# A second MoE layer with seven products: work of the other engines reordered around the products, squares moved to ACT, last step of each pass plain

## The chip, the cores and the metric

The kernel runs on one core of a Trainium2 chip. The metric is the device time of one execution in microseconds; the median of three runs is given, and one more execution was profiled. PE is the matrix engine (PEld its weight loads), DVE, ACT and POOL are the vector, scalar and GpSimd engines, SP issues nearly all DMAs. Each engine, and SP's queue, works off its instructions in program order.

## The reference

```python
# attention with two head-mixing matrices, then two feed-forward layers on 1792 tokens
s = mix(softmax_input = scale * q @ k.T, w_pre);  a = mix(softmax(s), w_post);  x = a @ v
h = x @ moe_w_in                                   # 768 -> 1024
solu = h * softmax(h);  ln = (solu - mean) / std * g_ln
x2 = ln @ moe_w_out                                # 1024 -> 768
h = x2 @ moe2_w_in                                 # 768 -> 2048
r = np.maximum(h, 0.0);  g = r * r
out = g @ moe2_w_out                               # 2048 -> 768
```

The weights of both feed-forward layers arrive as 64-bit floats.

## The kernel before, in words

The program has four stages: attention; the first MoE (`h1`, `norm1`, `zt`, `out1`), in tiles of 128 tokens for the way in and groups of 384 for the way out; a last loop of ten `out1` without `h1`, beside which the second MoE's first data are prepared; and the second MoE, which the change is about. All fp32 products are made of three matmuls each: an operand is split into a high part (a rounding copy on ACT) and a low part (a subtraction on DVE or POOL), and hi·hi, hi·lo and lo·hi are summed in PSUM.

The 64-bit weights are narrowed to fp32 by `narrow`: one square on ACT (line 75) and four operations on DVE (76, 80, 84, 88) for each piece of 128 x 384, then a store to DRAM (737) and the load of the piece after the next. A second-MoE weight has 64 pieces. They are put in small portions between other work: each call of `filler()` issues one DVE operation. The square's scratch tile (`wsq`) has one buffer, so the square of a piece waits for line 88 of the piece before. A loop of the first MoE issues 12 fillers in one batch ahead of its two `out1`, the last loop 5 after each `out1`, and each step of the second MoE up to 8.

The second MoE works in two passes p over tokens, of 1024 and of 768, each in two token groups q (`GRP`: 512 and 512, then 512 and 256), and in each pass over eight blocks of 256 hidden columns. `it` counts the 16 blocks of both passes, `e` the one within its pass; a step is a pair (it, q). A step has two parts on PE:

- `h2(it, q)`: 2 hidden tiles f x 6 chunks x 3 = 36 matmuls (line 916) of 512 or 256 columns. Relu on ACT (924) and the square on DVE (925, reading PSUM again) give `r`.
- `y2(it, q)`: g is cut in 2 x 2 blocks (hidden tile x token half), the weight block in 2 x 2 (hidden tile x half of the 768 outputs). Instead of eight block products there are seven, of sums of blocks: `s1..s4` on POOL (943), `t1..t4` on DVE (889). Each of the seven is 6 matmuls of 384 columns (3 for the group of 256 tokens; line 1020) into one of three PSUM buffers, and is then added to an fp32 sum `y` in SBUF by DVE (1031), or copied by ACT where e is 0 (1029). At the end of a pass `join` (seven DVE additions per group, line 983) turns the seven sums into the four output blocks. Only the very last block, `plain(it)`, has eight products into four sums of two.

PE's order is h2 of the next step, then y2 of this one, and so on; `h2(next)` is issued with 4 fillers after each hidden tile. After it, still ahead of this step's y2, a step with q = 0 issues `sum_to` (four DVE subtractions), two `split_to` and the four `split_ti` (ACT copy 829, POOL 830) of the next block, for which only two raw buffers `tir` exist, so that two of their loads wait for the first two splits. Splits of g (954, 955) are issued with or after h2 for k = 0 and 1 and in the `hook` between products for the rest; the splits of `to` (897, 898) likewise for k = 2 and more. The tokens `x2` are loaded and split in two halves of three chunks (801, 802), those of the second pass during block 7; both `join`s of a pass are worked off in one stretch at the next step with q = 0.

Of the kernel before, what the change touches and what calls it, by code (L numbers as in the profile page):

```python
# [18 lines left out]
def kernel(  # L19
# [726 lines left out]
    for m in range(NTILE):  # L746
# [76 lines left out]
    def split_ti(it, j):  # L823
# [3 lines left out]
        hi, lo = [ti[it, f][:, a, 3 * s:3 * s + 3] for a in range(2)]  # L827
        r = tir.pop((it, j)).rearrange("p (c f) -> p c f", c=3)
        nc.scalar.copy(hi, r)  # L829
        nc.gpsimd.tensor_tensor(out=lo, in0=r, in1=hi.bitcast(F32), op=ALU.subtract)  # L830

    def ahead():

        load_ti(0, 0)
        load_ti(0, 1)
        for half in range(2):
            yield from part_x2(0, 0, half, wi2_p)
        for j in range(4):
# [9 lines left out]
    for i, (g, cc) in enumerate(outs):  # L848
# [22 lines left out]
    def load_to(it):

        b = []
        for j in range(4, 8):
            i = 8 * (it % NE) + j
            need(i + 1)
            t = m2_p.tile([128, HM], F32, tag="tor", name="tor", bufs=4)
            nc.sync.dma_start(out=t, in_=w2D[i * 128:(i + 1) * 128, :])
            b.append(t)
        bsrc[it] = b  # L880

    def sum_to(it):
        b11, b12, b21, b22 = bsrc[it]
# [4 lines left out]
        for o, x, y in ((t1, b12, b11), (t2, b22, t1), (t3, b22, b12), (t4, t2, b21)):  # L888
# [17 lines left out]
    def plain(it):  # L906
        return it == NI - 1

    def h2(it, q, nf):
        n = GRP[it // NE][q][1]  # L910
        rs = []
        for f in range(KE):
            ps = ps2_p.tile([128, 512], F32, tag="h", name="ps_h2", bufs=2)
            for cc in range(CC):
                for i, (w, a) in enumerate(((0, 0), (0, 1), (1, 0))):
# [3 lines left out]
                        rhs=x2[it // NE, q][cc // 3][:, a, cc % 3, 0:n],  # L919
# [25 lines left out]
        split_g(it, q, 0)  # L945
        split_g(it, q, 1)

    def split_g(it, q, k):
        if k >= len(gsrc[it, q]):
            return  # L950
        r = gsrc[it, q][k]
        w = GRP[it // NE][q][1] // 2
        t = m2_p.tile([128, 2, TG // 2], F32R, tag="g", name="g", bufs=9)[:, :, 0:w]
        nc.scalar.copy(t[:, 0], r)
        (nc.vector if k < 2 else nc.gpsimd).tensor_tensor(  # L955
            out=t[:, 1], in0=r, in1=t[:, 0].bitcast(F32), op=ALU.subtract
        )
        gs.setdefault((it, q), []).append(t)
# [10 lines left out]
    def join(p, q):  # L969
# [3 lines left out]
        done = {}  # L973
        for o, x, y, op, c in (
            (p2, p1, p2, ALU.add, (0, 0)),
            (p6, p1, p6, ALU.add, None),
            (p7, p6, p7, ALU.add, None),
            (p6, p6, p5, ALU.add, None),
            (p5, p7, p5, ALU.add, (1, 1)),
            (p4, p7, p4, ALU.subtract, (1, 0)),  # L980
            (p3, p6, p3, ALU.add, (0, 1)),
        ):
            nc.vector.tensor_tensor(out=o, in0=x, in1=y, op=op)
            if c:
                done[c] = o
                if p == 0:
                    store_y(p, q, *c, o)
            yield True
        ys[p, q] = done

    def y2(it, q, hook):
        p, e = divmod(it, NE)
        na = GRP[p][q][1] // 256
        g = gs.pop((it, q))
        if plain(it):
            for (i, u) in ((0, 0), (0, 1), (1, 0), (1, 1)):
                ps = ps2_p.tile([128, 2, 512], F32, tag="y", name="ps_y", bufs=3)
                ab = [((g[0], g[1]), (g[3], g[2]))[i], ((to[it][0], to[it][1]), (to[it][3], to[it][2]))[u]]
                for a in range(na):
                    for f, (gg, tt) in enumerate(zip(*ab)):  # L1000
                        for j, (ga, wa) in enumerate(((0, 0), (0, 1), (1, 0))):
                            nc.tensor.matmul(
                                out=ps[:, a, 0:HM],
                                lhsT=gg[:, ga, a * 128:(a + 1) * 128],
                                rhs=tt[:, wa],
                                start=(f == 0 and j == 0),
                                stop=(f == KE - 1 and j == 2),
                            )
# [3 lines left out]
                hook(2 * i + u)  # L1012
            return
        if e == 0:
            ys[p, q] = [m2_p.tile([128, 2, HM], F32, tag=f"y{q}_{k}", name="y") for k in range(7)]
        for k in range(7):
            ps = ps2_p.tile([128, 2, 512], F32, tag="y", name="ps_y", bufs=3)
            for a in range(na):
                for j, (ga, wa) in enumerate(((0, 0), (0, 1), (1, 0))):
                    nc.tensor.matmul(  # L1020
                        out=ps[:, a, 0:HM],
                        lhsT=g[k][:, ga, a * 128:(a + 1) * 128],
                        rhs=to[it][k][:, wa],
                        start=(j == 0),
# [17 lines left out]
    for k in range(2, 7):  # L1042
        split_g(0, 0, k)
# [98 lines left out]
```

## Time and profile before

| | us |
|---|---|
| median of 3 runs (lowest, highest) | 1401.6 (1400.91, 1402.68) |
| profiled execution / its span | 1401.2 / 1399.3 |
| PE busy | 1211.3 (87%) |
| DVE / ACT / POOL busy | 903.3 / 571.9 / 572.5 |
| chain that ended last | PE 71%, DVE 10%, DMA 5%, POOL 5%, ACT 4%, issue 4% |

The profile's rows are read like this. A group's row gives the busy time, the mean length of one, and the idle time of that engine right before such instructions with what ended it. A timeline row gives start and length of a run of like instructions, and in brackets the idle time before it. The granted clock (PEclk) is a mean over a stretch between half speed, 0.5 for 1.2 GHz, and full speed, 1.0 for 2.4 GHz.

### The profile page before, as it was taken

How to read it: one execution, taken by the hardware profiler on the slowest of the kernel's cores; microseconds unless marked ns; L12 is line 12 of the kernel's file. 1: busy time of each engine (PE TensorE's matmuls, PEld its weight loads, DVE VectorE, ACT ScalarE, POOL GpSimd, SP SyncE). 2: the span in 40 equal slices, each digit the busy share in tenths (PEclk: the TensorE clock that was granted, in tenths of full speed). 3: DMA queues.
4: the chain of work that ended last, by engine and by line, in shares of the span. 5: the costliest groups of instructions: out<-in, count | busy, mean ns of one | idle time of the engine just before them, and what ended most of it. 6: DMA issues, size and time to landing. Idle time of an engine off the chain costs nothing.

```text
span 1399.3 us, 22134 instructions
## 1 busy us (share of the span) xinstructions
PE 1211.3 (87%) x7587; PEld 1012.0 (72%) x7587; DVE 903.3 (65%) x1649; ACT 571.9 (41%) x1445; POOL 572.5 (41%) x741
## 2 busy tenths in 40 slices
PE   9999999999999999999775776867798758777787
PEld 4777777777777889999764665756687547777777
DVE  4776777677757677777456367676655573555557
ACT  4565556666655442232233523232322234333331
POOL 2332232242215341110126646465557565566651
PEclk9999999999999999999888788987999878889998
DMA  6766665765636244444465223231211241111111
GB/s 182 223 187 185 196 195 175 201 202 168 199 123 191 80 141 147 147 147 125 151 205 157 74 63 100 83 93 51 79 45 41 81 142 38 50 46 45 48 44 68
DMA packets 131739, 172.19 MB, mean 123 GB/s; under 512 B 24492, under 2 KB 114220, under 8 KB 131628
## 3 DMA queue, kind: packets, MB, share of 16 engines
q1 hardware_dynamic: 130843, 170.51, 40.2%
q8 instruction: 61, 1.00, 0.3%
q14 instruction: 51, 0.41, 0.1%
q10 hardware_dynamic: 784, 0.27, 0.1%
HBM read 96.82 MB, written 35.39 MB: 94 GB/s over the span
## 4 chain that ended last, share of the span: by engine, by line
PE 71%; DVE 10%; DMA 5%; POOL 5%; ACT 4%; issue 4%; SPq 1%; DVEq 0%; ACTq 0%; POOLq 0%
PE ps_h L916 16%; PE ps_post L293 10%; PE ps_y L1020 10%; PE ps_pre L231 9%; PE ps_h L424 8%; PE ps_o L699 6%; PE ps_av L320 5%; PE ps_qk L204 5%; DVE tT L889 3%; DMA x2r<-x2D 2%; DVE g L955 1%; POOL s L943 1%; DVE r L925 1%; DVE y L1031 1%; ACT r L924 1%
## 5 line engine op out<-in xcount | busy, mean ns | idle before, releaser
L1020 PE MATMUL ps_y<-to,g 128*128 128x384 f32 x1113 | 251.6, 387 | 151.5 <-DVE y L1031 109.3
L1020 PEld LDWEIGHTS ps_y<-to,g 128*128 128x128 f32 x1113 | 234.0, 225 | 165.2 <-issue 70.5
L916 PE MATMUL ps_h<-x,ti 128*128 128x512 f32 (+1 forms) x1152 | 249.5, 375 | 9.7 <-ACT x L801 3.8
L916 PEld LDWEIGHTS ps_h<-x,ti 128*128 128x128 f32 x1152 | 205.2, 198 | 48.7 <-ACT x L801 6.0
L293 PEld LDWEIGHTS ps_post<-w,e 120*112 120x112 f32 (+1 forms) x1440 | 168.3, 177 | 67.8 <-issue 47.9
L307 DVE COPY at<-ps_post 112x480 f32<-112x480 f32 x180 | 117.2, 651 | 109.8 <-PE ps_post L293 109.3
L293 PE MATMUL ps_post<-w,e 120*112 120x120 f32 (+1 forms) x1440 | 182.6, 270 | 1.9 <-ACT w L280 1.5
L1031 DVE TENSOR_TENSOR y<-ps_y,y 128x768 f32<-128x768 f32 (+1 forms) x182 | 151.0, 857 | 30.8 <-PE ps_y L1020 28.1
L256 ACT ACTIVATE e<-ps_pre,nm 120x448 f32<-120x448 f32 x180 | 114.8, 638 | 131.5 <-POOL w L273 73.2
L231 PE MATMUL ps_pre<-sdst,wpre_bd 120*120 120x448 f32 x360 | 166.3, 545 | 0.8 <-ACT e L256 0.7
L925 DVE SCALAR_TENSOR_TENSOR r<-ps_h,r 128x512 f32<-128x512 f32 (+1 forms) x64 | 39.8, 625 | 190.5 <-ACT r L924 190.3
L699 PE MATMUL ps_o<-zt,w1o 128*128 128x384 f32 (+1 forms) x720 | 129.6, 341 | 18.3 <-ACT o L707 18.3
L273 POOL TENSOR_TENSOR w<-wpost_bd,sm 120x120 f32<-120x120 f32 x166 | 64.2, 407 | 187.8 <-DVE sm L267 176.9
L699 PEld LDWEIGHTS ps_o<-zt,w1o 128*128 128x128 f32 x720 | 124.8, 201 | 20.1 <-ACT o L707 20.1
L943 POOL TENSOR_TENSOR s<-r 128x256 f32<-128x256 f32 (+1 forms) x60 | 47.7, 795 | 220.3 <-DVE r L925 220.3
L924 ACT ACTIVATE r<-ps_h 128x512 f32<-128x512 f32 (+1 forms) x64 | 34.7, 544 | 211.3 <-PE ps_h L916 211.3
L424 PE MATMUL ps_h<-w1i,xs 128*128 128x512 f32 x504 | 119.2, 393 | 0.4 <-ACT xt L335 0.4
L244 DVE TENSOR_REDUCE nm<-ps_pre 120x1 f32<-120x448 f32 x180 | 110.1, 612 | 7.4 <-PE ps_pre L231 4.8
L424 PEld LDWEIGHTS ps_h<-w1i,xs 128*128 128x128 f32 x504 | 93.8, 188 | 20.0 <-ACT xt L335 0.6
L75 ACT ACTIVATE wsq<-wr 128x384 f32<-128x384 f32 x64 | 35.6, 556 | 167.2 <-DVE wt L88 102.9
L213 ACT COPY ssrc<-ps_qk 120x448 f32<-120x448 f32 (+1 forms) x186 | 85.1, 544 | 10.3 <-PE ps_qk L204 10.3
L830 POOL TENSOR_TENSOR ti<-tir,ti 128x384 fp32r<-128x384 f32 x64 | 70.6, 1112 | 40.4 <-ACT ti L829 40.1
(93 smaller groups left out, 1718.6 us busy)
## 6 DMA issues: line engine op xcount, KB each, us to landing
sdst<-ssrc SPq DMA_DIRECT2D x172, 210.0 KB
wr<-in_moe_w_in_dram SPq DMA_DIRECT2D x32, 384.0 KB
w2D<-wt SPq DMA_DIRECT2D x64, 192.0 KB
wr<-in_moe_w_out_dram SPq DMA_DIRECT2D x32, 384.0 KB
tir<-w2D SPq DMA_DIRECT2D x64, 192.0 KB
tor<-w2D SPq DMA_DIRECT2D x64, 192.0 KB
w1raw<-in_moe_w_in_dram SPq DMA_DIRECT2D x24, 256.0 KB
w1raw<-in_moe_w_out_dram SPq DMA_DIRECT2D x24, 256.0 KB
```

Source lines behind the costliest of these rows:

```text
L213: (nc.vector.tensor_copy if dve else nc.scalar.copy)(ssrc[c][0:n, h, :], ps[0:n, 0:S])
L231: nc.tensor.matmul(out=ps[0:m, 0:S], lhsT=wpre_bd[0:m].rearrange("p i g -> p (i g)")[:, 0:m], rhs=d[0:m], start=True, stop=True,)
L244: nc.vector.tensor_reduce(out=nm[0:m], in_=ps[0:m, 0:S], op=ALU.max, axis=AX.X, negate=True)
L256: nc.scalar.activation(out=e[0:m], in_=ps[0:m, 0:S], func=AF.Exp, bias=nm[0:m], scale=1.0, accum_out=sm[0:m])
L293: nc.tensor.matmul(out=ps[:, j, :, 0:r], lhsT=e[0:m, j * JW:(j + 1) * JW], rhs=w[0:m, :, 0:r], start=True, stop=True,)
L307: nc.vector.tensor_copy(at[c][:, :, :, oa:oa + r], ps[:, :, :, 0:r])
L424: nc.tensor.matmul(out=ps[:, u], lhsT=t[:, a, cc], rhs=w1i[cc][:, w, u * 512:(u + 1) * 512], start=(cc == 0 and a == 0 and w == 0), stop=( ...
L699: nc.tensor.matmul(out=ps[:, 0:width], lhsT=w1o[k][:, w, cc * 128:(cc + 1) * 128], rhs=zT[:, a, k, 0:width], start=(k == 0 and i == 0), st ...
L830: nc.gpsimd.tensor_tensor(out=lo, in0=r, in1=hi.bitcast(F32), op=ALU.subtract)
L916: nc.tensor.matmul(out=ps[:, 0:n], lhsT=ti[it, f][:, w, cc], rhs=x2[it // NE, q][cc // 3][:, a, cc % 3, 0:n], start=(cc == 0 and i == 0), ...
L1020: nc.tensor.matmul(out=ps[:, a, 0:HM], lhsT=g[k][:, ga, a * 128:(a + 1) * 128], rhs=to[it][k][:, wa], start=(j == 0), stop=(j == 2),)
L1031: nc.vector.tensor_tensor(out=yo, in0=po, in1=yo, op=ALU.add)
```

## The change

- The second pass has its groups in the order 256, 512 instead of 512, 256. `plain` holds for the last block of each pass. The `join`s are called in full, one per step, ahead of the last block's y2.
- Squares go to ACT (`AF.Square` on r in place).
- Each step issues, ahead of `h2(next)`: the low parts of g for k = 0, 1 (DVE); for q = 0 the `to` splits 2..6 and two `ti` splits (ACT, POOL); for q = 1 two `ti` low parts (now DVE), `sum_to` and two `to` splits; then 11 (q = 0) or 5 (q = 1) fillers, 4 more in the first block. After `h2(next)`: two `ti` copies and one `tor` load (q = 0) or four `tir` loads (q = 1), then y2, whose hook only splits g; three `tor` loads after it. In the second pass DVE takes the low parts of `to` for k = 0, 1 (before: odd k).
- `tir` has four buffers (two), `x2r` three (two); x2 tiles are pairs of chunks, loaded one by one further ahead.
- Where e is 0, ACT copies the even products and DVE the odd ones (before: ACT all).
- In the first MoE 5 fillers are issued in the batch and 4 after each `out1` (before: 12 in the batch); in the last loop 3 (before: 5) with fewer x2 steps beside them.

```diff
-        for _ in range(12 if m > GT else 0):
+        for _ in range(5 if m > GT else 0):
             filler()
...
             if outs:
                 out1(*outs.pop(0))
+                for _ in range(4):
+                    filler()
...
-    GRP = [[(0, 512), (512, 512)], [(1024, 512), (1536, 256)]]
+    GRP = [[(0, 512), (512, 512)], [(1024, 256), (1280, 512)]]
...
-        tir[it, j] = wi2_p.tile([128, 384], F32, tag="tir", name="tir", bufs=2)
+        tir[it, j] = wi2_p.tile([128, 384], F32, tag="tir", name="tir", bufs=4)
...
-        for _ in range(5):
+        for _ in range(3):
             filler()
         next(beside, None)
-        next(beside, None)
+        if i % 2:
+            next(beside, None)
...
-        return it == NI - 1
+        return it % NE == NE - 1
...
             nc.scalar.activation(out=r[:, 0:n], in_=ps[:, 0:n], func=AF.Relu)
-            nc.vector.scalar_tensor_tensor(
-                out=r[:, 0:n], in0=ps[:, 0:n], scalar=0.0, in1=r[:, 0:n], op0=ALU.max, op1=ALU.mult
-            )
+            nc.scalar.activation(out=r[:, 0:n], in_=r[:, 0:n], func=AF.Square)
...
-            if e == 0:
+            if e:
+                nc.vector.tensor_tensor(out=yo, in0=po, in1=yo, op=ALU.add)
+            elif k % 2:
+                nc.vector.tensor_copy(yo, po)
+            else:
                 nc.scalar.copy(yo, po)
...
+        if q and nxt:
+            for j in (2, 3):
+                ti_lo(it + 1, j, nc.vector)
+        for k in range(2):
+            lo_g(it, q, k, nc.vector)
+        if q == 0:
+            split_to(it, 2, 7)
+            if nxt:
+                for j in range(2):
+                    ti_hi(it + 1, j)
+                    ti_lo(it + 1, j, nc.gpsimd)
+        elif nxt:
+            sum_to(it + 1)
+            split_to(it + 1, 0, 2)
+        if e == NE - 2 and q == 1:
+            join(p, 0)
+        if e == NE - 1 and q == 0:
+            join(p, 1)
+        if p == 0 and e == NE - 1:
+            if q == 0:
+                for c in range(0, CC, 2):
+                    split_x2(1, 0, c, nc.vector)
+                    load_x2(1, 1, c // 2)
             else:
+                for c in range(3):
+                    split_x2(1, 1, c, nc.vector)
+                    load_x2(1, 1, c + 3)
+        for _ in range((5 if q else 11) + (4 if it == 0 else 0)):
             filler()
+        if more:
+            h2(*steps[i + 1])
+
+        if q == 0:
+            if nxt:
+                for j in (2, 3):
+                    ti_hi(it + 1, j)
+                load_to(it + 1, B[3])
+        elif it + 2 < NI:
             for j in range(4):
+                load_ti(it + 2, j)
+        if it == NE - 2 and q == 1:
+            for c in range(0, CC, 2):
+                load_x2(1, 0, c)
 
         def hook(k):
+            if more:
+                g = gs[steps[i + 1]]
+                hi_g(*steps[i + 1])
+                if len(g) > k + 2:
+                    lo_g(*steps[i + 1], k + 2, nc.gpsimd)
+            if it == NE - 1 and q == 1 and k < 3:
+                split_x2(1, 1, k + 3, nc.gpsimd)
 
         y2(it, q, hook)
+        if q and it + 2 < NI:
+            for fu in B[:3]:
+                load_to(it + 2, fu)
```

## Rows read from the trace of the kernel before

**Rows 1.** Windows by stage: start:end, length, busy us per engine, PEclk, DMA share, GB/s.

```profile
510.00:650.00 140.00, 140.00 (x739) 127.67 (x738) 108.06 (x179) 41.02 (x79) 19.03 (x24) 1.00 0.46 144
668.50:731.10 62.60, 44.28 (x249) 42.73 (x249) 29.98 (x53) 17.61 (x37) 13.08 (x10) 0.84 0.60 185
731.10:783.84 52.74, 29.88 (x116) 23.68 (x115) 26.40 (x36) 22.15 (x48) 32.98 (x33) 0.77 0.42 129
783.84:830.33 46.49, 35.96 (x158) 32.05 (x157) 26.27 (x34) 19.49 (x41) 26.31 (x30) 0.85 0.27 85
830.33:1022.86 192.53, 141.66 (x625) 127.44 (x625) 133.40 (x167) 55.39 (x131) 103.34 (x114) 0.86 0.26 80
1022.86:1103.19 80.33, 68.38 (x313) 61.31 (x313) 43.77 (x53) 23.86 (x58) 50.35 (x59) 0.92 0.14 42
1103.19:1159.38 56.19, 35.77 (x157) 30.65 (x157) 33.90 (x42) 20.45 (x47) 31.64 (x36) 0.82 0.42 134
1159.38:1359.84 200.46, 161.71 (x812) 147.15 (x811) 108.08 (x162) 65.14 (x176) 116.80 (x150) 0.91 0.15 43
1359.84:1399.30 39.46, 30.30 (x166) 28.29 (x165) 26.06 (x40) 6.54 (x20) 8.99 (x12) 0.91 0.17 61
```

**Rows 2.** Groups by form on PE, second MoE (from 731 us).

```profile
L1020 PE MATMUL ps_y<-to,g 128*128 128x384 f32 x1113 | 251.6, 387 | 151.5 <-DVE y L1031 109.3 <-ACT y L1029 33.1 <-ACT to L897 9.0
L916 PE MATMUL ps_h<-x,ti 128*128 128x512 f32 x864 | 208.5, 398 | 8.2 <-ACT x L801 2.7 <-POOL x L802 2.6 <-DVE r L925 2.1
L916 PE MATMUL ps_h<-x,ti 128*128 128x256 f32 x288 | 41.1, 306 | 1.5 <-ACT x L801 1.0 <-POOL x L802 0.4
L1002 PE MATMUL ps_y<-to,g 128*128 128x384 f32 x72 | 12.7, 334 | 0.0
```

**Rows 3.** Timeline of PE, second MoE: start, length, then the instructions.

```profile
778.18 5.82 PE L1020 MATMUL ps_y<-to,g 128*128 128x384 f32 x24 [18.70 <-ACT y L1029]
...
899.94 8.46 PE L916 MATMUL ps_h<-x,ti 128*128 128x512 f32 x36
908.24 3.30 PE L1020 MATMUL ps_y<-to,g 128*128 128x384 f32 x18
920.40 6.34 PE L1020 MATMUL ps_y<-to,g 128*128 128x384 f32 x24 [8.86 <-DVE y L1031]
...
1034.83 4.40 PE L1020 MATMUL ps_y<-to,g 128*128 128x384 f32 x24 [0.50 <-DVE y L1031]
...
1255.79 5.95 PE L1020 MATMUL ps_y<-to,g 128*128 128x384 f32 x24 [3.58 <-DVE y L1031]
```

**Rows 4.** Timeline of DVE and POOL after an h2, block 4.

```profile
915.93 2.57 POOL L830 TENSOR_TENSOR ti<-tir,ti 128x384 fp32r<-128x384 f32 x2
916.42 1.23 DVE L889 TENSOR_TENSOR tT<-tor,tT 128x384 f32<-128x384 f32 x1
...
918.84 0.55 DVE L889 TENSOR_TENSOR tT<-tT,tor 128x384 f32<-128x384 f32 x1
```

**Rows 5.** Windows, tile wt (fillers), blocks 2 to 5: DVE busy, then clock, DMA.

```profile
830.33:1022.86 192.53, 40.15 (x62) 0.86 0.26 80
```

**Rows 6.** The same of tile y (evictions): DVE busy, ACT busy.

```profile
830.33:1022.86 192.53, 52.02 (x57) 0.00 (x0) 0.86 0.26 80
```

**Rows 7.** The same of tile g: PE, PEld, DVE, ACT, POOL busy.

```profile
830.33:1022.86 192.53, 77.05 (x337) 73.62 (x336) 15.28 (x16) 20.45 (x56) 27.61 (x38) 0.86 0.26 80
```

**Rows 8.** The same of tile tT: DVE, ACT, POOL busy.

```profile
830.33:1022.86 192.53, 17.76 (x16) 8.11 (x16) 16.82 (x16) 0.86 0.26 80
```

**Rows 9.** Waits by engine in the last loop of the first MoE (668 to 731).

```profile
PE ps_o L699 <- ACT o L707: 18.3, 6, 5.2
```

**Rows 10.** Groups by form on ACT, second MoE.

```profile
L1029 ACT COPY y<-ps_y 128x768 f32<-128x768 f32 x21 | 16.8, 805 | 1.7 <-PE ps_y L1020 1.6
...
L801 ACT CAST x<-x2r 128x512 fp32r<-128x512 f32 x10 | 6.2, 618 | 14.7 <-DMA x2r<-x2D 14.7
```

**Rows 11.** Waits by engine, second MoE: total us, times, longest.

```profile
ACT wsq L75 <- DVE wt L88: 39.8, 19, 2.4
```

More of the change, by code (lines that the diff above doesn't have):

```diff
@@ L868, with plain, load_to @@
     to = {}
+    b = {}
     bsrc = {}
[L871 to L880, printed above, removed]
+    def plain(it):
+        return it % NE == NE - 1
+    def load_to(it, fu):
+        i = 8 * (it % NE) + 4 + 2 * fu[0] + fu[1]
+        need(i + 1)
+        t = m2_p.tile([128, HM], F32, tag="tor", name="tor", bufs=4)
+        nc.sync.dma_start(out=t, in_=w2D[i * 128:(i + 1) * 128, :])
+        b[it, fu] = t
     def sum_to(it):
-        b11, b12, b21, b22 = bsrc[it]
+        b11, b12, b21, b22 = [b.pop((it, fu)) for fu in ((0, 0), (0, 1), (1, 0), (1, 1))]
         if plain(it):
@@ L993, in y2 @@
         na = GRP[p][q][1] // 256
-        g = gs.pop((it, q))
+        g, t = gs.pop((it, q)), to[it]
         if plain(it):
@@ L997, in y2 @@
                 ps = ps2_p.tile([128, 2, 512], F32, tag="y", name="ps_y", bufs=3)
[L998 to L1008, printed above, removed]
+                gg, tt = ((g[0], g[1]), (g[3], g[2]))[i], ((t[0], t[1]), (t[3], t[2]))[u]
+                product(ps, na, list(zip(gg, tt)))
                 yo = ys[p, q][i, u]
@@ L1012, in y2 @@
                 hook(2 * i + u)
+            hook(4)
             return
@@ L1017, in y2 @@
             ps = ps2_p.tile([128, 2, 512], F32, tag="y", name="ps_y", bufs=3)
[L1018 to L1024, printed above, removed]
-                        stop=(j == 2),
-                    )
-            yo, po = ys[p, q][k][:, 0:na], ps[:, 0:na, 0:HM]
@@ L1028, in y2 @@
-            if e == 0:
-                nc.scalar.copy(yo, po)
-            else:
-                nc.vector.tensor_tensor(out=yo, in0=po, in1=yo, op=ALU.add)
-            hook(k)
-        if plain(it + 1) or e == NE - 1:
-            fill2.append(join(p, q))
-    steps = [(it, q) for it in range(NI) for q in range(len(GRP[it // NE]))]
-    rest = part_x2(0, 1, 1, m2_p)
-    next(rest)
-    load_to(0)
-    h2(*steps[0], 0)
-    run(rest)
-    for k in range(2, 7):
-        split_g(0, 0, k)
-    sum_to(0)
@@ L1045 @@
-    for k in range(7):
-        split_to(0, k)
-    for i, (it, q) in enumerate(steps):
-        nxt = it + 1 < NI
-        if q == 0 and nxt:
-            load_ti(it + 1, 0)
-            load_ti(it + 1, 1)
-            load_to(it + 1)
-        while q == 0 and fill2:
-            filler()
-        nw = []
-        if it == NE - 1:
-            nw = [part_x2(1, q, half, (m2_p if q and half else wi2_p)) for half in range(2)]
-            next(nw[0])
-        if i + 1 < len(steps):
-            h2(*steps[i + 1], 4)
-        if q == 0 and nxt:
-            sum_to(it + 1)
-            split_to(it + 1, 0)
-            split_to(it + 1, 1)
+            product(ps, na, [(g[k], t[k])])
@@ L1081 @@
         y2(it, q, hook)
-        for part in nw:
-            run(part)
+        if q and it + 2 < NI:
+            for fu in B[:3]:
+                load_to(it + 2, fu)
     ps2.__exit__(None, None, None)
```

201 lines of the change are left out of this document (112 added, 89 removed).

## The prediction

> **What bounds the kernel now.** I read the windows by stage first, then PE's groups and timeline, then who was busy during PE's waits.
>
> The windows [rows 1] show where time can be had. In the first MoE's main loop PE is busy all 140 us at a granted clock of 1.00; nothing is to be gained there. From 668.5 us on, PE is busy 44 of 62.6 us, and in the second MoE (731 to 1399) between 57% and 85% of each stretch, at clocks of 0.77 to 0.92. So the change works in the one part of the program where PE waits. The cuts of the windows lie where `h2(it, 0)` begins; I call the stretch from there to the next such start a pair (one y2 with q = 1, one h2 with q = 1, one y2 with q = 0, one h2 with q = 0). Blocks 2 to 5 take 192.5 us, 48.1 each; blocks 9 to 14 take 200.5, 33.4 each.
>
> What a pair needs of PE alone: a matmul of y2 without waits costs 12.7 / 72 = 0.176 us, an h2 of 256 columns 36 x 41.1 / 288 = 5.1 us [rows 2], an h2 of 512 columns 8.46 [rows 3]. A pair of the first pass is 2 x 8.46 + 84 x 0.176 = 31.7 us, one of the second 8.46 + 5.1 + 63 x 0.176 = 24.7. The differences, 16.4 and 8.7 us, are waits and half clock. PE's idle time is nearly all in one place: 151.5 us ahead of y2 matmuls, 109.3 of them until DVE's eviction of y and 33.1 until ACT's, against 9.7 ahead of both h2 forms [rows 2].
>
> The timeline shows how [rows 3]. After h2, 18 matmuls (three products, one for each PSUM buffer) run in 3.30 us; then PE stands 8.86 us for the first eviction, and the other 24 take 6.34 instead of 24 x 0.176 = 4.2, because the clock has gone to its lower level. After a wait of 0.50 they take 4.40, after one of 3.58, 5.95. A wait of some us thus costs about 1.7 us more.
>
> Why the eviction is late: DVE's queue holds, ahead of it, the second square (which waits for h2 to end), fillers, two g splits and four `tT`, and all these run beside POOL. A `tT` takes 1.23 us while POOL's split of `ti` runs and 0.55 alone [rows 4]. DVE is not full: 133.4 of 192.5 us in blocks 2 to 5 [rows 1]. The order is the limit, and the fillers and sums come after h2 where they should run beside it.
>
> **The change, part by part.** The sum is against the profiled execution, 1401.2 us (span 1399.3 and 1.9 around it), 0.4 under the median of 1401.6.
>
> *First pass, blocks 1 to 5.* DVE's work per pair now: 40.15 / 4 = 10.0 for fillers [rows 5], 52.0 / 4 = 13.0 for evictions (0.91 each) [rows 6], 15.3 / 4 = 3.8 for g [rows 7], 17.8 / 4 = 4.4 for `tT` [rows 8]; squares make the rest of the 33.4 in [rows 1]. The squares (about 2.5) go to ACT; two `ti` low parts of some 1.1, the mean of a `tT` in [rows 8], come. DVE then holds 33 us per pair, slightly more than PE's 31.7: the pair cannot go below 33 while fillers last, and they last for 96 calls (64 pieces x 4, less 160 issued in the first MoE): 15, 9, then 11 and 5 per block, into block 5.
>
> Now the order. Ahead of y2's evictions, DVE has everything queued behind nothing but earlier work, so it starts about 1 us into h2 (when the last eviction ends). The first eviction must be done before product 4: 8.46 + 3 x 1.06 = 11.6 us after h2's start. That leaves 11.6 - 1.0 - 0.9 = 9.7 us. With q = 0, 13 operations stand there (2 g, 11 fillers). Clean, at 0.55, they need 7.2 us; all beside POOL, at 1.23, 16. POOL has five `to` and two `ti` splits there, so I take 7 slow and 6 at 0.6: 12.2 us, a wait of 2.5. With q = 1 there are 13 again (2 `ti`, 2 g, 4 `tT`, 5 fillers), but POOL has only two `to` and what is left of g: 4.5 slow, 8.5 clean, 10.6 us, a wait of 0.9. With 2 us of half clock after the longer wait and 2 for what I don't see (fillers waiting for their load, uneven evictions) a pair is 31.7 + 3.4 + 2 + 2 = 39. Bounds: 33 and 46. Block 1 has 9 fillers instead of 5 and ACT evictions at e = 0: 42 against 46.5. Blocks 2 to 4 at 39 and block 5 at 37: 154 against 192.5. Together **-43**.
>
> *Last blocks of the first pass (6 to 8).* Block 6 has no fillers: 33. Block 7 gains 6 plain matmuls (1.05 us) and seven join operations ahead of an eviction: 36. Together 69 against 80.3: **-11.3**. Block 8 now stands at 56.2, for both joins run in one stretch and the x2 splits come in the middle of h2 [rows 1]. Its PE work will be 5.1 + 48 x 0.176 + 8.46 + 3.7 = 25.7. Ahead of y2(7, 1), DVE has 13 operations, with half slow some 11.5 us, and 5.1 + 6.3 - 1.9 = 9.5 to do it in (a plain product is 12 matmuls). With 2 + 2 for that, 2 for the last x2 chunks, which POOL splits between products, and 2 for ACT's evictions: 34. **-22** (bounds 28 and 45).
>
> *Second pass, blocks 9 to 14.* The tight spot is q = 1 again, for its h2 has only 256 columns: 10 operations (2 `ti`, 2 g, 4 `tT`, 2 `to`) in 5.1 + 3.2 - 0.5 - 0.9 = 6.9 us. Clean they need 5.5, half slow 9.2: a wait of 2.3, and 1 us of clock: 28 against 33.4. Bounds: 25 and 31. Six blocks: **-32.5**.
>
> *Block 15 and the end.* PE: 42 x 0.176 + 5.1 + 8.46 + 72 x 0.176 = 33.6; join ahead of the last evictions, 4; 3.4 after PE's last matmul as now, with a larger last store. 41 against 39.5: **+1.5** (-2 to +5).
>
> *The last loop of the first MoE.* PE waits 18.3 us for ACT's copy of `ps_o` [rows 9], since ACT stands ahead of it for x2 chunks and pieces to arrive: DMA moves 185 GB/s over 62.6 us, 11.6 MB [rows 1]. With 3 instead of 5 fillers the loop narrows 7.5 pieces instead of 12.5; a piece is 384 KB in and 192 KB out, so about 2.9 MB less. At the same rate that is 15 us; I take **-12** (-4 to -18), since the loads still stand in one queue with the x2 stores. In the main loop 13 fillers replace 12 for each tile; DVE is busy 108 of 140 us there, and PE has two `out1` in between: nothing.
>
> *Start of the second MoE (block 0).* Now 52.7 us, 18.7 of them one wait for ACT's evictions [rows 3]. After the change DVE has four x2 splits, four `tT`, two g and 15 fillers ahead, and ACT's eviction stands behind the filler squares. The last x2 chunk can arrive only some 15 us in; DVE's 21 remaining operations at 0.8 and 2 us of DMA bring ACT to 37, and four products follow at half clock: 45. **-7.5** (-15 to +2).
>
> *Squares on ACT.* From SBUF, 512 columns: a cast of that size takes 0.62 [rows 10]; bounds 0.3 and 1.0. ACT is busy 55 of 192 us; its spare time hides it. If the cover were gone it would be 4 x 0.62 per pair. More doubtful is ACT's order: a filler's square waits for DVE's line 88 (39.8 us in all now [rows 11]), and with eleven fillers ahead of h2 the Relu stands behind the third square, up to 11 us into h2 instead of 4.2. Behind it wait the squares, the sums of POOL and the g splits, some 10 us in all; they are needed only 24 us after h2's start. So this costs nothing until the Relu slips past 14 us. Four `tir` buffers, loads a step earlier, three x2r buffers: their waits were ACT's, mostly off the path; at nothing, covered by 10 us of lead.
>
> Sum: -43 - 11.3 - 22 - 32.5 + 1.5 - 12 - 7.5 = -126.8, so 1274.4 by the profiled execution, **1275** in the measure of the median.
>
> **A rule weighed.** The rows on `tT` show a DVE operation of two SBUF inputs slowed from 0.55 to 1.23 beside POOL [rows 4]. The Trainium skill (SBUF — State Buffer, "SBUF: two separate sides") says that such a DVE operation and a POOL instruction that reads SBUF exclude each other for the whole instruction. By it, a pair with fillers holds 22 such DVE operations of 0.55 and POOL's 103.3 / 4 - 2.2 = 23.6 us [rows 1], an estimate of 35.7 at the least. The trace agrees only in part: POOL's two took 2.57 with two DVE operations between. It leaves the 39 as they are and lifts the next rival by some 8 us.
>
> **The rivals.**
> *Nearly all waits go* (16%): 34 for blocks 2 to 5, 36 for block 1, 66 for 6 and 7, 29 for 8, 25.5 for the second pass, 38 at the end, 40 at the start, -17 in the last loop: 187 less, 1214. For it: clean DVE operations fit in every gap. Against: POOL is busy more than half of the time, and DVE has no slack while fillers last.
> *The waits move* (27%): eleven fillers in one burst meet POOL throughout and their own loads, DVE is late by 5 us or more in each step: 45 for blocks 2 to 5, 46.5 for block 1, 74, 42, 31 for the second pass, 43 at the end, 50 at the start, -6 in the loop: 53 less, 1348. For it: a `tT` beside POOL took twice its clean time [rows 4], most fillers read two SBUF operands as it does, and each burst waits for its own loads. Against: nothing on DVE waits for h2's end any more.
> *The clock stays low* (6%), the slower side: shorter waits come at every product, and y2 runs at half speed throughout. That adds 14 x 1.06 = 14.8 us to a pair of the first pass and 11.1 to one of the second: 49.5 for blocks 2 to 5, 97 for 6 and 7, 42, 37.3, 57 at the end, 49.5 and 50 for blocks 1 and 0, -6 in the loop, +43, **1444**. It turns the sum to slower once about 55% more of the y2 matmuls run low than I allow (127 of 227 us). Against it: the wait of 0.50 us left 24 matmuls at 4.40 [rows 3].
> The Trainium skill (TensorE: Matmul & The Clock Gate, "A second HAM failure mode: psum-queue depth-cycling") warns of this: short idles between matmul groups that cycle PSUM buffers can make the clock swing. The clock of 0.92 in blocks 6 and 7 [rows 1], which cycle the same buffers, speaks against it here.
> *No effect* (2%): the waits are kept by something that I don't see, such as SP's queue.
>
> **How the numbers follow.** Forecast 49%, with its own range 1240 to 1315. For 8 in 10 I go from 1225, into the first rival, to 1350, to the middle of the second; what is left out is half of the first rival, a part of the second and the slower ones. A difference of 0.2% (2.8 us) is about what can be told from none. Faster 0.91, the same 0.02, slower 0.07.
>
> **What would show it.** Per pair, h2 to h2: 39 in blocks 2 to 4, 33 in block 6, 28 in the second pass; PE's idle ahead of y2 down from 151 to some 50 us, mostly still until DVE, at q = 0 in the first pass and at q = 1 in the second; clock above 0.9 from block 2 on; the first h2 at about 719. Wrong it would be if PE waited for POOL's or ACT's g instead, or if DVE's operations ahead of y2 took over 1 us on average.

## The result, and the profile after

The changed kernel takes **1237.85 us** (median of 4 runs, 1237.23 to 1239.83), 0.8833 of the kernel before (95% interval 0.8817 to 0.8848). The forecast was 1275 within 1225 to 1350: the direction and the mechanism hold, the gain of 164 us is 37 larger than the 127 forecast, and the time lies 2 us below the forecast's own range. The profiled execution has a span of 1235.5 us.

Windows of the changed kernel, cut like those of before [rows 1] (last loop of the first MoE; block 0; 1; 2 to 5; 6 and 7; 8; 9 to 14; 15 and the end); columns as there:

```profile
668.50:720.20 51.70, 41.42 (x261) 40.85 (x261) 31.77 (x50) 17.27 (x37) 13.80 (x12) 0.87 0.64 201
720.20:765.17 44.97, 29.35 (x116) 23.01 (x115) 29.70 (x33) 21.70 (x48) 29.57 (x30) 0.81 0.49 150
765.17:800.53 35.36, 31.95 (x158) 27.96 (x157) 29.09 (x40) 20.12 (x44) 20.98 (x25) 1.00 0.39 129
800.53:941.05 140.52, 131.26 (x625) 117.98 (x625) 126.44 (x158) 64.14 (x149) 95.09 (x111) 0.95 0.34 110
941.05:1004.65 63.60, 63.50 (x320) 57.21 (x319) 49.02 (x59) 28.39 (x63) 32.82 (x39) 1.00 0.26 82
1004.65:1030.99 26.34, 25.38 (x143) 22.94 (x142) 14.80 (x24) 13.92 (x36) 19.62 (x25) 1.00 0.58 195
1030.99:1190.77 159.78, 147.70 (x812) 136.66 (x811) 114.23 (x152) 78.78 (x201) 116.64 (x148) 0.97 0.20 58
1190.77:1235.50 44.73, 34.73 (x187) 32.21 (x186) 31.31 (x41) 9.13 (x24) 11.15 (x13) 0.95 0.15 54
```

Against the forecast, in us:

| stretch | before | forecast | after | gain forecast | gain measured |
|---|---|---|---|---|---|
| last loop, up to the first h2 | 731.1 | 719 | 720.2 | 12 | 10.9 |
| block 0 | 52.7 | 45 | 45.0 | 7.5 | 7.8 |
| block 1 | 46.5 | 42 | 35.4 | 4.5 | 11.1 |
| blocks 2 to 5 | 192.5 | 154 | 140.5 | 38.5 | 52.0 |
| blocks 6, 7 | 80.3 | 69 | 63.6 | 11.3 | 16.7 |
| block 8 | 56.2 | 34 | 26.3 | 22 | 29.9 |
| blocks 9 to 14 | 200.5 | 168 | 159.8 | 32.5 | 40.7 |
| block 15 and the end | 39.5 | 41 | 44.7 | -1.5 | -5.3 |

Groups by form on PE, changed kernel from 700 us; line 999 is now all products, the plain ones too. The answers to [rows 2]:

```profile
L999 PE MATMUL ps_y<-to,g 128*128 128x384 f32 x1197 | 233.1, 352 | 45.3 <-DVE y L1029 26.9 <-DVE y L1031 15.3 <-ACT y L1033 1.1
L930 PE MATMUL ps_h<-x,ti 128*128 128x512 f32 x864 | 204.9, 394 | 1.7 <-ACT x L807 1.1 <-DVE x L808 0.5
L930 PE MATMUL ps_h<-x,ti 128*128 128x256 f32 x288 | 35.7, 283 | 0.0
```

PE's idle time ahead of y2 fell from 151.5 to 45.3 us; it is still DVE's eviction that ends nearly all of it. The timeline of PE, for comparison with [rows 3]: start of the second MoE, block 3, a block of the second pass, block 15:

```profile
758.47 2.26 PE L999 MATMUL ps_y<-to,g 128*128 128x384 f32 x6 [13.17 <-DVE y L1031]
...
851.72 8.50 PE L930 MATMUL ps_h<-x,ti 128*128 128x512 f32 x36
860.06 3.30 PE L999 MATMUL ps_y<-to,g 128*128 128x384 f32 x18
866.53 7.10 PE L999 MATMUL ps_y<-to,g 128*128 128x384 f32 x24 [3.16 <-DVE y L1029]
873.47 8.32 PE L930 MATMUL ps_h<-x,ti 128*128 128x512 f32 x36
881.63 7.47 PE L999 MATMUL ps_y<-to,g 128*128 128x384 f32 x42
...
1118.81 4.43 PE L999 MATMUL ps_y<-to,g 128*128 128x384 f32 x24 [2.41 <-DVE y L1029]
...
1203.29 5.97 PE L999 MATMUL ps_y<-to,g 128*128 128x384 f32 x24 [4.90 <-DVE y L1029]
```

With q = 1 all 42 matmuls now run in one piece, 7.47 us; with q = 0 the break of 8.86 us is one of about 3. Why the two differ is in the timeline of the other engines in block 3 (q = 0 from 851.7, q = 1 from 873.5):

```profile
855.08 1.17 DVE L76 TENSOR_SCALAR wt<-wr 128x384 uint32<-128x384 uint32 x1
856.27 1.25 DVE L80 SCALAR_TENSOR_TENSOR wt<-wr,wt 128x384 uint32<-128x384 uint32 x1
857.07 1.32 POOL L915 TENSOR_TENSOR to<-tor,to 128x384 fp32r<-128x384 f32 x1
...
861.22 0.56 DVE L80 SCALAR_TENSOR_TENSOR wt<-wr,wt 128x384 uint32<-128x384 uint32 x1
...
863.97 0.36 DVE L76 TENSOR_SCALAR wt<-wr 128x384 uint32<-128x384 uint32 x1 [0.93 <-DMA wr<-in_moe_w_in_dram]
...
864.40 0.58 ACT L938 ACTIVATE r<-ps_h 128x512 f32<-128x512 f32 x1
...
865.43 2.68 DVE L1029 TENSOR_TENSOR y<-ps_y,y 128x768 f32<-128x768 f32 x3
...
876.76 1.01 DVE L907 TENSOR_TENSOR tT<-tor 128x384 f32<-128x384 f32 x2
...
882.88 7.21 DVE L1029 TENSOR_TENSOR y<-ps_y,y 128x768 f32<-128x768 f32 x7 [1.40 <-PE ps_y L999]
```

At q = 0 the same filler takes 1.25 us while POOL splits `to` and `ti`, and 0.56 when it has ended; DVE's 13 operations take from 852.8 to 865.4, a wait of 0.93 us for the load of a filler's piece included. At q = 1 POOL is idle for most of h2, two `tT` take 1.01 us together, and DVE waits 1.40 us for PE ahead of its first eviction: here DVE is early.

### The profile page after: what moved, and what is told of

Its sections match the earlier page's. It is cut to its first block, busy times and chain, and to the rows that moved or that the text cites. A ratio compares the mean times of both kernels' runs of the same rounds, so it can differ in the third digit from the quotient of the medians.

```text
span 1235.5 us, 22011 instructions
## 1 busy us (share of the span) xinstructions
PE 1167.3 (94%) x7599; PEld 975.5 (79%) x7599; DVE 899.6 (73%) x1612; ACT 594.8 (48%) x1485; POOL 527.3 (43%) x696
## 5 line engine op out<-in xcount | busy, mean ns | idle before, releaser
L999 PE MATMUL ps_y<-to,g 128*128 128x384 f32 x1197 | 233.1, 352 | 45.3 <-DVE y L1029 26.9
L999 PEld LDWEIGHTS ps_y<-to,g 128*128 128x128 f32 x1197 | 221.3, 199 | 54.2 <-ACT r L938 24.6
L930 PE MATMUL ps_h<-x,ti 128*128 128x512 f32 (+1 forms) x1152 | 240.7, 366 | 1.7 <-ACT x L807 1.1
L930 PEld LDWEIGHTS ps_h<-x,ti 128*128 128x128 f32 x1152 | 197.7, 189 | 38.3 <-DVE x L808 2.0
L1029 DVE TENSOR_TENSOR y<-ps_y,y 128x768 f32<-128x768 f32 (+1 forms) x168 | 139.2, 854 | 65.3 <-PE ps_y L999 60.6
L75 ACT ACTIVATE wsq<-wr 128x384 f32<-128x384 f32 x64 | 35.6, 556 | 210.6 <-DVE wt L88 123.4
L699 PE MATMUL ps_o<-zt,w1o 128*128 128x384 f32 (+1 forms) x720 | 124.8, 334 | 11.3 <-ACT o L707 11.3
L699 PEld LDWEIGHTS ps_o<-zt,w1o 128*128 128x128 f32 x720 | 120.9, 196 | 12.5 <-ACT o L707 12.4
L953 POOL TENSOR_TENSOR s<-r 128x256 f32<-128x256 f32 (+1 forms) x56 | 42.0, 751 | 109.9 <-ACT r L939 109.9
L968 POOL TENSOR_TENSOR g<-s,g 128x256 fp32r<-128x256 f32 (+1 forms) x112 | 83.3, 764 | 6.1 <-ACT g L964 5.1
L938 ACT ACTIVATE r<-ps_h 128x512 f32<-128x512 f32 (+1 forms) x64 | 34.5, 539 | 105.1 <-PE ps_h L930 105.1
L320 PEld LDWEIGHTS ps_av<-at,v 112*64 112x64 f32 x1536 | 73.8, 137 | 12.2 <-ACT ssrc L213 5.3
```

Of the source, the lines that this page charges most:

```text
L699: nc.tensor.matmul(out=ps[:, 0:width], lhsT=w1o[k][:, w, cc * 128:(cc + 1) * 128], rhs=zT[:, a, k, 0:width], start=(k == 0 and i == 0), st ...
L930: nc.tensor.matmul(out=ps[:, 0:n], lhsT=ti[it, f][:, w, cc], rhs=x2[it // NE, q][cc // 2][:, a, cc % 2, 0:n], start=(cc == 0 and i == 0), ...
L968: eng.tensor_tensor(out=t[:, 1], in0=gsrc[it, q][k], in1=t[:, 0].bitcast(F32), op=ALU.subtract)
L999: nc.tensor.matmul(out=ps[:, a, 0:HM], lhsT=g[:, ga, a * 128:(a + 1) * 128], rhs=t[:, wa], start=(f == 0 and j == 0), stop=(f == len(pairs ...
L1029: nc.vector.tensor_tensor(out=yo, in0=po, in1=yo, op=ALU.add)
```

## The experiments

The expectations name the theories. "Place": what counts is how long DVE's queue is between its last eviction of one y2 and the first of the next, against the cover that h2 and three products give. Gains and losses below are differences of the ratios to the kernel before, times 1402 us; the changed kernel's ratio is 0.8833.

**Fillers 8 and 8.** `range((5 if q else 11) + ...)` becomes `range(8 + ...)`.

> The changed kernel with 8 fillers in either step of a block instead of 11 (q = 0) and 5 (q = 1). Theory 'place' (what counts is how many us DVE's queue holds between its last eviction of one y2 and the first of the next, against 9.7 us of cover): in blocks 2 to 5 of the changed kernel DVE's work ahead of y2 takes 12.6 us at q = 0 and 8 us at q = 1; with 8 and 8 it is about 10 and 9.5, the waits of 2.7 to 3.2 us and the 1.6 us of half clock behind them go to under 1: 4 blocks x 4, 1222 us (1215 to 1230). Rival 'load' (DVE's total of 33 us per pair is the limit, not its place): no change, 1235 to 1241.

Ratio 0.8743 (0.8726 to 0.8759), 12.6 us less. Blocks 2 to 4 go from 35.7, 37.2 and 35.6 to 33.6, 32.8 and 32.8, block 0 from 45.0 to 41.9 (3 fillers less ahead of its y2); block 5 gets 0.8 longer. So blocks 2 to 5 give 8.6 us, about half of the 16 expected there, and block 0 gives 3.0 that were not expected. In PE's timeline the break at q = 0 of block 3 is now

```profile
859.26 4.43 PE L999 MATMUL ps_y<-to,g 128*128 128x384 f32 x24 [1.37 <-ACT g L964]
```

and the matmuls behind it run at full clock. (ACT's g is named, but it ended at 859.28, after these matmuls had started; DVE's first eviction started at 858.17 and took 0.9: it is DVE still.) The wait is not under 1 us as expected: at q = 0 all 8 fillers now run beside POOL. The window of blocks 2 to 5 is

```profile
797.19:929.06 131.87, 125.76 (x625) 112.31 (x625) 127.14 (x161) 63.32 (x147) 96.18 (x110) 1.00 0.37 117
```

DVE's total work is what it was (127.1 us, before 126.4), so "load" falls as the limit of the changed kernel; with DVE busy 96% of this window it is the next one.

**The first `to` splits a step earlier in the second pass.** A new function splits k = 0, 1 from the raw tiles; it is called at q = 0, behind the `ti` splits, where `split_to(it + 1, 0, 2)` falls away.

```diff
+                if it >= NE:
+                    split_first(it + 1)
         elif nxt:
             sum_to(it + 1)
-            split_to(it + 1, 0, 2)
+            if it < NE:
+                split_to(it + 1, 0, 2)
```

> The changed kernel with the two first splits of to for the next block moved, in the second pass, from the step with q = 1 to the step with q = 0, where DVE stands idle for 6 us. Theory 'place': DVE's work ahead of y2 at q = 1 falls from 8.3 to 6.7 us, the wait of 2.42 us to about 0.9, with some half clock less: 6 blocks x 2.3, 1224 us (1219 to 1231). Rival 'shared' (what DVE does ahead of y2 is set by POOL's activity, and moved operations are slowed as much elsewhere or slow POOL's splits): 1235 to 1242.

Ratio 0.8724 (0.8702 to 0.8746), 15.3 us less. Five blocks of the second pass now take 24.8 to 24.9 us, 1.2 more than block 9, where PE does not wait (23.6). PE's timeline, the same step as the 2.41 us above:

```profile
1113.06 4.40 PE L1007 MATMUL ps_y<-to,g 128*128 128x384 f32 x24 [0.94 <-DVE y L1037]
```

Two operations of 0.8 us moved took 1.5 us off the wait and with it all half clock. At their new place they take 2.66 us beside POOL, and nobody waits for them. "Shared" falls. Block 8 pays 1.9 us (28.2 instead of 26.3): there ACT's part of the moved splits waits 5.75 us for the load of `tor`.

**Both edits.**

> Both edits (fillers 8 and 8; first two splits of to a step earlier in the second pass). Theory 'place': they lie in different blocks and add up, 1208 us (1198 to 1220). Rivals 'load' and 'shared': 1232 to 1242.

Ratio 0.8672 (0.8654 to 0.8691), 22.6 us less of the 27.9 that the two make singly. Blocks 9 to 14 keep nearly all of theirs (11.3 of 11.9 us). But the kernel with the early splits alone also had 34.5 and 34.0 us in blocks 3 and 4, 4.3 less than the changed kernel, where its edit touches nothing: half clock that did not come, and that the other edit removes as well. In block 3 of the kernel with the early splits the break was as long as in the changed kernel, and the matmuls behind it took 4.40 us instead of 7.10:

```profile
868.09 4.40 PE L1007 MATMUL ps_y<-to,g 128*128 128x384 f32 x24 [3.16 <-DVE y L1037]
```

**Squares back on DVE.** The `AF.Square` line is replaced by line 925 of the kernel before.

> The changed kernel with the squares back on DVE, reading PSUM as before; all else as changed. Theory 'place': DVE gets 2 x 0.69 us ahead of the evictions; at q = 0 of blocks 1 to 5 that adds 1.4 and some half clock, at q = 1 the square ends before the first eviction could start anyway, in the second pass 6 x 1: 1250 us (1243 to 1262). Rival 'squares' (the gain comes from no DVE instruction waiting for h2's end any more): with that wait back most of the old waits return, 1290 us or more.

Ratio 0.8895 (0.8882 to 0.8909), 8.7 us more. Two rows of its timeline, DVE at q = 0 and q = 1 of the same block:

```profile
869.79 1.28 DVE L939 SCALAR_TENSOR_TENSOR r<-ps_h,r 128x512 f32<-128x512 f32 x2
...
887.60 0.69 DVE L939 SCALAR_TENSOR_TENSOR r<-ps_h,r 128x512 f32<-128x512 f32 x1 [0.98 <-ACT r L938]
```

At q = 0 the squares add their 1.28 us to a queue that is late anyway, the wait grows to 4.17; at q = 1 DVE waits 0.98 us for h2's end, as the rival says, but PE does not wait. The squares' move is a small part of the gain.

**Fillers behind h2.** The filler loop is moved below `h2(*steps[i + 1])`.

> The changed kernel with the fillers issued behind h2(next) instead of ahead of it. DVE's order stays the same, since h2 now issues nothing on DVE; on ACT the fillers' squares fall behind the four Relu and square instructions of h2. Theory 'place': the first line 88 of a burst then waits for h2 to end (9.9 us into it instead of 7), the rest of the burst runs without POOL beside it: the first eviction some 1 to 2 us later at q = 0 and 0.5 too late at q = 1, with half clock 3 us per block, more in block 0: 1252 us (1244 to 1264). Rival 'squares' (fillers tied to h2's end through ACT bring the old waits back): 1280 or more. If the order on ACT does not matter: 1235 to 1241.

Ratio 0.9056 (0.9043 to 0.907), 31 us more: above the range of "place" and under that of "squares". Blocks 1 to 5 take 43.9, 41.1, 41.2, 41.1 and 40.2. The mechanism is the expected one, with a larger size:

```profile
876.90 1.02 DVE L88 SCALAR_TENSOR_TENSOR wt<-wsq,wt 128x384 f32<-128x384 f32 x1 [4.32 <-ACT wsq L75]
...
884.39 6.00 PE L999 MATMUL ps_y<-to,g 128*128 128x384 f32 x24 [6.74 <-DVE y L1029]
```

DVE's instruction order is the same, but line 88 needs ACT's square, which now stands behind the second Relu; DVE idles 4.32 us in the middle of its burst. Place must be read on the engine that feeds DVE, too.

**The last loop as before.** `range(3)` becomes `range(5)` and the second `next(beside, None)` is unconditional.

> The changed kernel with the last loop of the first MoE as before (5 fillers and two x2 steps after each out1). Theory 'DMA' (that loop is bound by bytes): its end moves from 720 to about 730 us, as before; 20 fillers less are left for the second MoE, so blocks 4 and 5 lose their fillers and save 3 us each: 1242 us (1236 to 1249). Rival (the loop's gain comes from the x2 tiles being loaded with three buffers and one by one): the loop ends at 720 to 723, and the fillers that it takes away make 1229 to 1236.

Ratio 0.8892 (0.8879 to 0.8905), 8 us more. The loop ends at 737.4 instead of 720.2; blocks 3 to 5, with no fillers left at the end, take 34.1, 31.2 and 31.1 and give 8.4 back. PE in the loop:

```profile
708.73 8.49 PE L699 MATMUL ps_o<-zt,w1o 128*128 128x256 f32 x48 [6.38 <-ACT o L707]
...
732.08 5.49 PE L699 MATMUL ps_o<-zt,w1o 128*128 128x256 f32 x24 [4.77 <-ACT o L707]
```

The window of this loop:

```profile
668.50:737.37 68.87, 46.82 (x261) 45.54 (x260) 42.46 (x67) 19.85 (x42) 17.26 (x14) 0.81 0.62 193
```

That is 13.3 MB at 193 GB/s, against 10.4 MB at 201 in the changed kernel; five pieces are the 2.9 MB between them, and the 17 us for them 170 GB/s. The kernel before moved 11.6 MB in its loop, which fits that this one ends 6 us later than that one, and not at the 730 expected. The rival is out and "DMA" holds; fillers and x2 steps were put back together here, not one by one. The fillers cost less in the second MoE than in a loop bound by bytes.

**Seven products in block 7 too.** `plain` is `it == NI - 1`; the joins and stores of the first pass come at (7, q = 1) and (8, q = 0).

> The changed kernel with seven products in the last block of the first pass too (only the very last block is plain), its joins and stores one step later. PE has 12 matmuls less, 2.1 us. Theory 'place': DVE gets two sums, seven evictions more and a join ahead of a short h2 of 256 columns (20 operations, 15 us, against about 7 of cover), so blocks 7 and 8 get 6 to 10 us of waits: 1244 us (1239 to 1254). Rival 'matmuls' (the sums hide): 1233 to 1238.

Ratio 0.8912 (0.8882 to 0.8942), 11 us more. Block 7 gains 1.4 us, block 8 goes from 26.3 to 41.8:

```profile
1014.51 7.01 PE L999 MATMUL ps_y<-to,g 128*128 128x384 f32 x24 [8.34 <-DVE y L1029]
...
1035.32 1.30 PE L999 MATMUL ps_y<-to,g 128*128 128x384 f32 x3 [3.88 <-DVE y L1031]
```

12 matmuls more on PE bought a block without joins in DVE's way.

**Squares on ACT alone, in the kernel before.** Line 925 is replaced by `AF.Square` on ACT.

> The kernel before with one part of the change alone: squares on ACT, reading r. Theory 'place': DVE's second batch of four fillers no longer waits for h2's end, but the g splits do (through ACT), and the four sums stand behind them: 2.6 us less wait in some eleven steps with fillers, little in the second pass: 1375 us (1360 to 1390). Rival 'squares' (this was the wait that counted): 1320 or less.

Ratio 0.9818 (0.9801 to 0.9834), 25.5 us less, as expected: blocks 1 to 5 take 215 instead of 239 us, blocks 9 to 13 some more than before. In that order of work the square held four fillers back until h2's end, so the same move was worth 25 us there and 9 in the changed kernel.

**Fillers and sums ahead of h2, in the kernel before.** Eight fillers and, at q = 0, `sum_to` are issued ahead of `h2(*steps[i + 1], 0)`; the second kernel has the squares on ACT besides.

> The kernel before with its fillers (8 per step) and the four sums of sum_to issued ahead of h2(next); squares stay on DVE, all else as before. Theory 'place': four fillers and four sums leave the stretch between h2's end and the first eviction; the second square and the g splits, which wait for h2's end, stay there. At q = 0 the eviction comes 2.5 us earlier, at q = 1 also, with less half clock 6 us per block in 1 to 5, and 4 in the second pass: 1347 us (1330 to 1365). Rival 'squares' (DVE waits for h2's end all the same, so only the squares' move can help): 1380 or more.

> Both parts in the kernel before: fillers and sums ahead of h2, and squares on ACT. Theory 'place': only the two g splits are left behind h2's end, the first eviction comes about 3 us (q = 0) and 1 us (q = 1) late: some 39 us per block in 1 to 5 and 29 to 30 in the second pass: 1328 us (1308 to 1345). Rival 'feeds' (the loads further ahead and the POOL splits ahead of h2 carry the rest of the gain, so these two parts alone stay well above): 1350 or more.

Ratios 0.9704 (0.9679 to 0.973) and 0.9767 (0.9749 to 0.9785): 41 and 33 us less. The first is near "place" (1361 against 1347), the second misses (1370 against 1328) and lies where the rival "feeds" has it; adding the squares' move made it 9 us slower. Timeline of the second, from q = 1 of one block into q = 0:

```profile
885.20 13.61 SPq L878 DMA_DIRECT2D tor<-w2D  x4
...
900.87 0.56 DVE L889 TENSOR_TENSOR tT<-tor,tT 128x384 f32<-128x384 f32 x1 [4.93 <-DMA tor<-w2D]
...
910.49 1.69 DVE L953 TENSOR_TENSOR g<-r,g 128x256 fp32r<-128x256 f32 x2 [2.21 <-ACT g L952]
...
913.19 6.87 PE L1018 MATMUL ps_y<-to,g 128*128 128x384 f32 x24 [7.82 <-DVE y L1029]
```

The sums now stand where DVE can do them early, but their data is not there: the issue of the `tor` loads drags on for 13.61 us, since their buffers are still read by the last `to` splits (POOL's last ends at 898.46), and with the sums all fillers wait behind them in DVE's queue. The same step of the first of the two:

```profile
895.84 0.56 DVE L889 TENSOR_TENSOR tT<-tor,tT 128x384 f32<-128x384 f32 x1 [5.09 <-DMA tor<-w2D]
...
904.55 1.28 DVE L955 TENSOR_TENSOR g<-r,g 128x256 fp32r<-128x256 f32 x2
...
906.85 5.76 PE L1020 MATMUL ps_y<-to,g 128*128 128x384 f32 x24 [7.33 <-ACT ti L829]
```

It waits for the load as long, but with the squares on DVE the low parts of g follow without a wait, where they wait 2.21 us for ACT in the other; PE's break is 0.5 us shorter. That accounts for a part of the 9 us; the rest was not followed up. The second pass gains next to nothing (32.9 for 33.4 per block in the first of the two). What carries the rest of the change's gain, the loads further ahead, the `to` splits ahead of h2 or something else in it, was not run by itself.

**Joins of the second pass later,** on top of both edits: the first at q = 0 of block 15, the second behind y2(15, 0).

> The changed kernel with fillers 8 and 8, the early splits of to, and the joins of the second pass one step later each (the first at q = 0 of the last block, the second behind that step's y2). Theory 'place': the wait of 4.9 us and half clock in y2(14, 1) go, some 2 us come back ahead of the last y2: 4 us under the kernel with the two edits alone, ratio to the kernel before 0.864 (0.861 to 0.867). Rival: the wait moves whole to the last y2, 0.867 to 0.870.

Ratio 0.8685 (0.8668 to 0.8702), nothing gained against 0.8672. The break in y2(14, 1) is gone and stands in the last y2 instead:

```profile
1203.64 10.33 PE L1007 MATMUL ps_y<-to,g 128*128 128x384 f32 x46 [7.09 <-DVE g L976]
```

The low parts of the last g stand behind the second join on DVE (6.5 us from 1196.7). The rival holds.

**No more than 8 fillers in block 0,** on top of that.

> The same, and no 4 additional fillers in the steps of block 0 (they come 8 later, in block 6). Theory 'place': block 0, where DVE and ACT's eviction stand behind the fillers, loses 3 to 4 us of waits, block 1 about 2, block 6 gains 2: 4 us less, ratio 0.861 (0.857 to 0.865). Rival (block 0 waits for the x2 loads and splits, not for the fillers): no change against the kernel without this edit.

Ratio 0.865 (0.8633 to 0.8667), 1212.7 us: the fastest version run, 2.1% under the changed kernel and 4.9 us under the one without this edit, 4 expected; it lies at the upper end of the expected range, which counted on the late joins as well. Blocks 0 and 1 take 38.7 and 32.0 instead of 40.9 and 36.2, and block 6 nothing more. Block 0's wait for DVE falls from 9.78 us in the kernel with both edits to

```profile
753.55 6.00 PE L1007 MATMUL ps_y<-to,g 128*128 128x384 f32 x24 [7.67 <-DVE y L1039]
```

What is left there is behind the x2 splits, the sums and the eight fillers that remain.

## Why the prediction was right, and where its sizes were off

**The main step holds.** PE waits for DVE's eviction of y, and the wait is set by what is queued ahead of it on DVE. The budget of 9.7 us with 13 operations gave a wait of 2.5 us at q = 0; the 13 took 12.2 to 12.6 us in blocks 2 to 4 (12.2 forecast), and the waits in blocks 2, 3 and 4 are 2.71, 3.16 and 2.76. In the second pass 10 operations in 6.9 us gave 2.3; five of the six blocks have 2.41 or 2.42. PE's idle time ahead of y2 is 45.3 us, forecast at some 50. The edits that shift operations between steps (8 and 8, early `to`) move the time the way that budget says.

The sizes were nearly all too cautious, and 37 us of gain is what this adds up to. The range of 1225 to 1350 held because it reached into the first rival.

**Term too small: blocks 1 to 5, 43 us of gain instead of 63.** Two parts of the 39 us pair were padding. The wait of 0.9 us at q = 1 did not come, for POOL is idle there: the mean of `tT`, 1.11 us in [rows 8], is 0.56 (tile tT, windows of the changed kernel, blocks 2 to 5; DVE busy first):

```profile
800.53:941.05 140.52, 8.99 (x16) 7.01 (x16) 18.12 (x16) 0.95 0.34 110
```

The 2 us "for what I don't see" did not come on top either: the waits for a filler's load are there (0.93 us in block 3), but inside these 12.6 us. PE alone needs 31.1 us (block 6, which has no wait); waits of 2.7 to 3.2 and 1.5 to 2.7 of half clock bring blocks 2 to 4 to about 36. Blocks 1 and 5 hold 11.6 of the 20 us:

```profile
796.29 4.40 PE L999 MATMUL ps_y<-to,g 128*128 128x384 f32 x24 [1.30 <-DVE y L1029]
...
936.81 4.40 PE L999 MATMUL ps_y<-to,g 128*128 128x384 f32 x24 [0.64 <-ACT ti L834]
```

In block 1 (35.4 against 42) the same 11 fillers cost only 1.30 us, since ACT does the last eviction of y2(0, 1), DVE begins at the start of h2 instead of 1.1 us into it, and its 13 operations take 11.8 us; in block 5 (32.0 against 37) eight fillers are left. Neither has half clock. The fillers, in turn, got slower (tile wt, the same stretch, against 40.15 in [rows 5]):

```profile
800.53:941.05 140.52, 46.22 (x61) 0.95 0.34 110
```

0.76 us each for 0.65, since at q = 0 about half of the eleven meet POOL: DVE's total of 126 us in 140 is what the forecast had as 33 per pair (31.6), and it did not bind.

**Blocks 6 and 7, 11.3 instead of 16.7.** Block 6 takes 31.1 and not 33, and block 7 takes 32.5 and not 36: the timeline shows no break in their y2, and y2(6, 1), behind a join, takes 7.81 us instead of 7.47.

**Block 8, 22 instead of 30.** Four allowances of 2 us (the wait ahead of y2(7, 1), half clock, x2 chunks, ACT's evictions) were not needed: PE waits 0.96 us in the whole block.

**Second pass, 32.5 instead of 40.7.** Block 9 makes 4.4 of the 8.2 us: it has no break at all,

```profile
1035.29 7.48 PE L999 MATMUL ps_y<-to,g 128*128 128x384 f32 x42
```

since ACT shares the evictions of y2(8, 1). In the others, an h2 of 256 columns takes 4.3 to 4.5 us, not 5.1: the mean that I read from [rows 2] held matmuls at half clock. And two of the five breaks ran on at full clock.

**Block 15, -1.5 instead of -5.3.** The join ahead of y2(14, 1) costs 4.90 us of wait and half clock behind it, more than the 4 that stood there, and 4.5 us instead of 3.4 follow PE's last matmul.

**The last loop, 12 instead of 10.9.** The number is near by some luck: 10.4 MB at 201 GB/s instead of 11.6 at 185 are 1.2 MB less, not the 2.9 of the working, and the rate is higher.

**What the prediction passed over** is that "loads a step earlier, at nothing" may be what lets DVE's work stand ahead of h2. The term did no harm to the sum. In the two orders tried in the kernel before, without the loads, 41 and 33 us of the gain come, and about 5 us of DMA wait stand at the head of DVE's queue. That the loads alone would bring the rest is not shown.

**ACT's order** came out nearly as told: at q = 0 the Relu starts 12.7 us into h2 (864.40), later than the 11 of the prediction but under the 14 at which it would have begun to cost, and the breaks of PE's matmuls name DVE. (The weight loads ahead of five of these breaks name that Relu, 24.6 us in all; they need nothing from it, it only came last.)

**The rivals.** "The waits move" is out (1348, and 45 us in blocks 2 to 5 where 35.1 were measured on average), and so are "no effect" and "the clock stays low": the granted clock is 0.95 to 1.00 from block 1 on. (That last rival's 227 us for all y2 matmuls at the lower level do not come out of the rows: 1197 of 0.176 us would add 211.) The rule weighed put a pair at 35.7 us at the least; blocks 2 to 4 came out near that, but it is no floor, for with fillers 8 and 8, and the same operations, blocks 3 to 5 take 32.8.

What a break costs in clock is not decided by its length alone. In the changed kernel the 24 matmuls behind 1.30 us or less ran 4.40, behind 2.41 to 2.42 twice 4.43 and three times 5.9 to 6.0, behind 2.7 to 4.9 always 5.9 to 7.1. In other kernels they ran 4.40 behind 3.16 us (above) and 5.97 behind 1.80, with the squares back on DVE:

```profile
1128.72 5.97 PE L1001 MATMUL ps_y<-to,g 128*128 128x384 f32 x24 [1.80 <-DVE y L1031]
```

With both edits the second pass is at the first rival's 25.5 or under; the whole kernel, 1212.7 in its best version, reaches that rival's 1214, but only with these further edits.

## What to carry to other kernels

Count, for the engine that frees PE's buffers, the operations queued between its last release and the next, and set them against the cover in PE's own time; do it for each step of a loop, since one step may be 3 us late while the next has 3 us to spare, and moving three operations per block across bought 12.6 us here without making any faster. DVE work that stands ahead of an eviction belongs where POOL is idle: here the same operation took 0.56 or 1.25 us. An operation can only move ahead if its data and its feeder (a load, a square on another engine) move ahead with it.

## What the runs showed of the hardware

A break in PE's work of about 2.4 us led to half clock in some blocks and not in others of the same kernel (4.43 or 5.9 us for the same 24 matmuls), and the same break of 3.16 us in block 3 was followed by 7.10 in the changed kernel and by 4.40 in the one with early `to` splits. So two kernels with equal waits can differ by 1.5 to 2.7 us per block, and a gain of that size in one block of one profile is no proof of an edit's effect. DVE operations with one SBUF source are slowed beside POOL as well: line 76 took 1.17 us there and 0.36 alone.
